# A fused recurrence and mixer on one core: the first low-rank product into two of four row groups, the second product for two chunks abreast, and a new order

## The chip, the cores and the metric

The kernel runs on one core of one Trainium2 chip (trn2). The metric is the time of one execution on the device in microseconds (us); the kernel before took 160.7 us, the median of three runs (160.70, 162.46 and 157.32).

## The reference

Four batches are computed, each with a sequence of 768 steps, 8 heads of width 48, so a model width of 384. A gated linear recurrence feeds a token mixer of rank 32 and a channel mixer with a hidden width of 1536:

```python
for t in range(S):                                    # S = 768
    state = alpha[:, :, t, :, None] * state + einsum('bhd,bhe->bhde', k[:, :, t], v[:, :, t])
    y[:, :, t] = einsum('bhd,bhde->bhe', q[:, :, t], state)
...
x = y as (batch, 768, 384)
h = x.transpose(0, 2, 1) @ U @ V                      # U: 768 x 32, V: 32 x 768
u = x + h.transpose(0, 2, 1)
out = u + maximum(u @ w_ch1, 0) @ w_ch2               # 384 x 1536 and 1536 x 384
```

## The kernel before

The sequence of each batch is cut into six chunks of 128 steps. Batches are numbered 0 to 3, and an operation is named here by its kind, its batch and its chunk (`mlp1 0.1.3`: batch 0, second half of the sequence, hidden block 3). Each batch goes through these stages:

- **Loads.** For each chunk one transfer each of alpha, k, q and v (192 KB) into one of 40 `io` tiles (`stage_loads`, lines 343 and 350). The weights of the channel mixer come over the same queue: twelve tiles of `w_ch1` of 192 KB (`weights1`, line 313), which are then cast into `w1_sb` by GpSimd or ScalarE (lines 265 and 269), and four pieces of `w_ch2` of 576 KB (`weights2`, line 328), which land in `h1t` and are cast from there into `w2_sb`. Three of the twelve tiles belong to one block of 384 hidden columns, that is to three of the twelve `mlp1` products of a half: tiles of block 0 to hidden blocks 0 to 2, of block 1 to 3 to 5, of block 2 to 6 to 8, of block 3 to 9 to 11.
- **Recurrence** (`stage_pair`, `stage_sums`, `stage_gla`). Logarithms of alpha are summed by a matmul (`pcum`, `cum`), exponentials of the sums scale k and q into `rkq` (`rk` and `rq`, lines 404 and 612, on GpSimd or VectorE), TensorE transposes these (`tr`, line 421), forms the scores (`psc`, `sc`), the state (`pd2`, `d`) and the result (`py`, `y`), and the result is copied from PSUM to `xb` (`pyev`, `yev`).
- **Token mixer** (`stage_mix`). The first low-rank product (`xu`, line 735) is one matmul for each of the six chunks, 128 rows by 32 columns, and it puts chunk c into column group c mod 4, so that one PSUM tile holds four partial sums of 32 rows each. One copy takes them to `utx` (128 x 384). The second product (`hb`, line 771) is one matmul per chunk over all 128 rows, against V repeated four times down the rows (`ve_sb`, `vm_sb`), so that this product also adds the four partial sums. VectorE adds the chunk of `xb` (`u`, line 772).
- **Channel mixer.** u is transposed, by TensorE in batches 0 and 1 (`utr`, line 791) and by the DMA queue in batches 2 and 3 (`tu`, line 777), then `mlp1` (line 820, three matmuls of 384 columns each), `relu` (lines 830 and 832), `mlp2` (line 846, twelve matmuls per chunk in three groups of four), the sum with u (line 852) and the store (line 857).

PSUM is used as eight banks. Each engine works through its own list in order, and waits at an instruction until what this needs is there. SyncE's list holds nearly all transfers. The order of all lists, the engine of each copy and the buffer of each tile are written out by hand: `Plan.add` collects the operations of all stages, and `Plan.run` issues them in the order of `TABLE`, three letters for one operation (two for its number, one for its engine), with `SLOTS` naming the buffers.

Of the kernel before, what the change touches and what calls it, by code (L numbers as in the profile page):

```python
# [13 lines left out]

CODE = "ABCDEFGHIJKLMNOPQRSTUVWXYZabcdefghijklmnopqrstuvwxyz0123456789+-"
TABLE = """
BDSA3AA7SA6AQLAA4SDeAA5SDgPBLSCXACZPBFSCuAA9SA8SCwPCYACaAAESCcACbADiAA+SCeDCzACyABESCdDEOAA-A++ECgPDlGCfPBHSCiDEQPBMSC1G
ChDDnPBGAETACxACmPDpABNSC0GCjPCnDDhABJSC3PERACkDAIGC2PCvABCACoPCqPClDC5AC9PDkGDFAC4DBASCpDESAC6PC+DBTSCrPEUGC7DC-PDmPBPA
DHPC8DDoADfGDBPBBSDIACsDEVGDCPDADDKADJADqPCtDBOSD3AEWPDDDDtPDEDDGGEXPDjADrDDUPD5PEZAEYDAJPD7ABIADuPDsDAKAEaPBKSDvDDLGEcD
BRSD+GGOABQADVPAMPGlADWDADSDNPDMGDwPD6AGQPDPDD8AANADXPDxDGnPGSADYDEPGDOPEbDGRABSSDyPD9GEdPDzPEAPGpADQDEePGoAD0PECDD4GGqA  # L20
DRPGTABUSD2AGVGD1AD-PEfDEgPBbADTDEGPEhPEBADZPEHPBVSDSDGUGDaPEDPBXSEIDDbPEEDAFGEiPBWADcAEKPGXPEkAEFDGWPDdAATSEJPGPAELPEjD
APSGYAGZDGdPGrGEMDElPARSENAGeDGaPHVAEmPGfDGhPGtPGbDEnAGsGAXSHXPGcDAVSEwPE2PHaAGvAE0PAZSExDGiPG8AEuPE1DBYSGmGGkAGuPGjAEqP
E3DAhSGwAEoPG+PEvDAdSAUAAQGE4PErDEpDAYGACGEyPEzDBaSBZSAfSAlSAjSG0PEsPAGPG1DAbSEtDASAHBAAaGAWGE5AFSPAAGHYAAHAG2DABDFUPG-A
HZAHAAFaPE6PFYPFCPFAPHCDFTAFZAFDDFVAFbAHEPFWPE7DHGDG9AHDGG3GE8PHFPE+PBjSFBAAgAAcAFEPFcPFFAAkAFXDE9DBfSBeSHHDHLPBcSBdSHIP
E-DGgGAmGBhSAnSBgSArSAvSAeGFiPFGPFIPHMDHNDAzSAOGHvAFdAHbGHRPFKPHJDAiAHKDFjAFHDHODHuAFJAHWABkSHcGFLDFmPFnDFkPFlABlSHQPHSP
HkPHUDHwPHlDHTAHmDHePHnDH1AIHAAqGHdPIGAApGHzAH0AHyAAoAH2GHfDHgAAsAAuGFoPFQPFpDFRDBrSBiSFePFgPFOPFhDFfAFPDFMPGxPHhPGzDHjD
AtAH3GBnSBmSBzSBoSFNAHiDHoGA0GBvSAxAAwAGIPAyGFwPH4PGyDH5PHpPGCPGJPHqPBpSH7AA1GH6DHPDH8PHrPF8PFxPIJDA2AF9PF+PH9DHtDH+DHxA
IIGILPHsDJ5AINAIKPIMDF-DFyPH-PFzDGKPJ6AIADIBDGDPGLDG4PIOPIPDIQDG5PJ7PJ+AJ9AKcAKOAKbAJ-AIDPIEDG6DKPAG7DBqSF2PICGIFGIRPISD
B3SGEPITPB1SBwSKdPF3PBxSGFDKMAIUAKNAB7SBySIjPKBGKCGKDSIkDALGKAABsSIbPIXPIVPF4PIdPKfAKwAKjGIWDIYDJ8AFqPKhAIhPFrPIZPIcDIeD
IfPKHPIiDIlPKiAKgAKxAKvAIaAKkGKyAFsPIgDI9PIxPIyAIrPIsAK+AF5DImDKIDI+DFtDK0DK-AJRPJSAJVPI-PJAAI5PI6AKQGJWDLAPLTABuSLSAKEP  # L30
KFDKGDKlSKmPLFALCAKLGJLPJFPKnDLEAB4SKeGLGGCHSJMALDAB5SLHDKWPKXDKoDCDSB2SB0SJHPJNPJJPJKDI3PI4DJODJIAB8SBtSKYGJPPI7PInPJDP
I1PKpPJGAI8AJEDKzDI2DLISB9SKJPKuAK1SKsPJBPKKAJCAIpPB6SNdAB-SM8AJQAIoAKtDIvPLUGKqDKrGIqAJTPK5PK6DJ0PJ1PKRGJvPLJPK2PJUDLKD
K3DLLDIzPI0AKSSK4DJ2PJwPJxPJyDIwAM7AItPLVGLBGLWSLMPK7GJ3DB+SK8PIuAK9ALNDLOGKTPM9PNAANRANBANCANQANOALXPJXPLPPLQACLSNeAKUD
KVDKZPJYPCESCMSLYDLZDLRGLaPJpPCASNSGCBSKaDLbALcPLdANfPJZPM-ANPANDGLjPN0ACGSNyALqPNzANkALlPNxACTSCFSLkDNEGN1GCCSNNAM+GLmD
LnSJqPLePLrDJrPLoPJjPJkPLfDLpDLsSLgPJdPJlPJePJfPN3PJsDN5ANYPNJPLhDJmDLiSCPSMTPMbPMVPNFSJgDNKDNTGNZDMUDNUSJaDMcDCJSCNSMWD
NhANiAMJPMKAODALvPLwACISLtPCQSMBPL7PLuDMCDOEAL8DMRPCVSMSANjANGPOFPNVPNHDNWDNIDObAOHAL9PL+ACKSOJACRSMLPMHPMIDMMAOaAMXPMNP
MFPL1PMODNmDNlDMYAL2ANnSL5PMZPMaAOIALzPMDPMGDN2GOLGNaGMPPL6DNXDMxPNgAONPN4PMQDNbPNrPN6DCUSNsDMEAL0AOKAL-PL3PMADCOSN7PNcA
OPDN9DNoPNpDFvSCSSJcSCWSN8DMyPL4ANwANLPOMGOdGOOPOfPLxPOQDOcGNMANtGLyAOePOgAMzPN+POBPORPOCAOGANqDOhDOiPN-DMiPOUPOTDOSDMjP
NuPM2POAGF7SOVDOZGOXPOjDNvAOkDOWGOlPM3POmAOYDOnPGHSFuSJnSGASJtSJuSF0SMsPMtPOoAOpPOrPOqDOuPMnPMkPOsDOtSOwPOvDMdPMlDOxDOyS
MePO1POzPO2DO0DM4PMuPMvDM0DMfPMoPMpPMqDM5DO4PPMPPGPPKPPOPO5APEPPLDPNAPFAJoSPPDMmSO3SJ4SMgDF6SPgPPcPPIPPQPPSPPdDPJAPTAPmP  # L40
PRAPnAPaPPkPO+PPbAPlAPUPPHAPVAMrSPWPPXDO6PPYPO7DPZDPhDMwSM6SJhSGBSJiSJbSJzSO8PO9DPCPPiPPAPPePO-APBAPjAPyPPtPP3PPoPPfAPDA
PzPPuPQBPGMSM1SP0PQCPMhSP1DF1SGNSP2SPpPQDPPvPPwDPxSPqPPrDPsSGGSQGPQHPQEDQIPQFSP4PQJDQKSP5PP6DP7SP8PP9PP+PP-DQAS
"""
# [94 lines left out]
def kernel(  # L138
# [42 lines left out]
    u_sb = const.tile([128, NC, R], BF16, name="u_sb")  # L181
# [3 lines left out]
    ue_sb = const.tile([128, NC, R], BF16, name="ue_sb")  # L185
# [148 lines left out]
    def paired(b, c):  # L334
        return c // 2 < PAIRS[b]
# [22 lines left out]
    def xk(b, xb, c):  # L358
        return [(xb, c, 0), (xb, c, 1)] if paired(b, c) else [(xb, c)]
# [369 lines left out]
    def stage_mix(b, xb, ub, uT):  # L729
        xu = Buf(bank)  # L730

        def f_utx(cs):
            for c in cs:
                g = c % 4
                nc.tensor.matmul(
                    xu()[32 * g : 32 * g + R, 0:DM], lhsT=(ue_sb if paired(b, c) else u_sb)[:, c, :], rhs=xb()[:, c, :],
                    start=(c < 4), stop=(c + 4 >= NC), skip_group_check=True,
                )
# [15 lines left out]
        def v_side(c):  # L754
            return (ve_sb if paired(b, c) else vm_sb)[:, c * C : (c + 1) * C]

        def f_hb3(c0):
            for g in range(3):
                rows = slice(32 * g, 32 * g + R)
                nc.tensor.matmul(hbs[c0 + g]()[:, 0:DM], lhsT=v_side(c0 + g)[rows], rhs=utx()[rows], start=True, stop=True)  # L760

        def v_keys(cs):
            return [("ve" if paired(b, c) else "vm", c // NT) for c in cs]

        for c in range(NC):
            hb = hbs[c]
            if b in ABREAST:
                if c % 3 == 0:
                    P.add(f"hb3 {b}.{c}", lambda e, c=c: f_hb3(c), r=[utx] + v_keys(range(c, c + 3)), w=hbs[c : c + 3])
            else:  # L770
                P.add(f"hb {b}.{c}", lambda e, c=c, hb=hb: nc.tensor.matmul(hb()[:, 0:DM], lhsT=v_side(c), rhs=utx(), start=True, stop=True), r=[utx] + v_keys([c]), w=[hb])  # L771
            P.add(f"u {b}.{c}", lambda e, c=c, hb=hb: nc.vector.tensor_tensor(ub()[:, c, :], xb()[:, c, :], hb()[:, 0:DM], op=ALU.add), r=[hb] + xk(b, xb, c), w=[(ub, c)])  # L772
# [144 lines left out]
```

## Time and profile before

| what | value |
|---|---|
| median of three runs | 160.7 us (157.32 to 162.46) |
| the profiled execution, its own time | 156.94 us |
| its span, first to last instruction | 155.0 us |
| what lies around the span | 1.94 us |
| TensorE busy | 146.3 us, 94% of the span, 1771 matmuls |
| VectorE, ScalarE, GpSimd busy | 109.1, 87.1 and 61.8 us |
| read from and written to HBM | 23.79 and 4.72 MB |

In the rows of the profile PE is TensorE, PEld its weight loads, DVE VectorE, ACT ScalarE, POOL GpSimd, and SPq the queue from which SyncE issues transfers. A row of the timeline has the start in us, the time from the first start to the last end of the merged instructions, the engine, the line, the operation with its tiles and shape, and how many were merged; in brackets stands how long the engine was idle before and what ended that. Matmuls overlap in TensorE's pipeline, so the pace of a stream is read from one start to the next and not from the length of one. A row of transfers has the line, the queue, the count, the size of one and the time from its issue to its landing.

### The profile page before, as it was taken

What the parts mean: (1) busy time and instruction counts of PE and PEld (TensorE: products, weight loads), DVE (VectorE), ACT (ScalarE), POOL (GpSimd) and SP (SyncE); (2) the same over time, 40 slices, a digit from 0 to 9 for tenths busy, and PEclk for the clock granted to TensorE, in tenths of its full rate; (3) what the DMA queues carried; (4) which work ended last, traced back from release to release, by engine and by line L of the source; (5) the groups of instructions that cost most, each with busy time, mean ns of one, the idle gap of its engine ahead of it and who ended that gap; (6) DMA issues with size and microseconds to landing.
All of it is one profiled execution on the core that took longest, in us unless ns stands there. A gap on an engine that the chain in (4) does not pass through costs nothing.

```text
span 155.0 us, 4552 instructions
## 1 busy us (share of the span) xinstructions
PE 146.3 (94%) x1771; PEld 97.6 (63%) x1771; DVE 109.1 (70%) x240; ACT 87.1 (56%) x225; POOL 61.8 (40%) x96
## 2 busy tenths in 40 slices
PE   0898999999999999999999999999999999999992
PEld 0567777666757675766657666666776555666661
DVE  6159999968989796879859665988897566160151
ACT  3858977988794549396636670775672103544000
POOL 8069886646557056254354473006553000000000
PEclk9999999999999999999999999999999999999999
DMA  4999999999998899999899997999984079760134
GB/s 120 323 325 323 270 287 343 307 340 244 338 351 183 183 209 228 159 221 230 151 216 198 184 234 133 199 204 187 191 210 121 9 172 160 240 218 0 51 125 161
DMA packets 94453, 32.35 MB, mean 209 GB/s; under 512 B 88128, under 2 KB 94400, under 8 KB 94432
## 3 DMA queue, kind: packets, MB, share of 16 engines
q1 hardware_dynamic: 89152, 30.09, 80.7%
q10 hardware_dynamic: 5280, 1.97, 4.9%
q8 instruction: 14, 0.23, 0.6%
q14 instruction: 7, 0.06, 0.1%
HBM read 23.79 MB, written 4.72 MB: 184 GB/s over the span
## 4 chain that ended last, share of the span: by engine, by line
PE 90%; DVE 5%; DMA 2%; issue 1%; POOL 1%; ACT 0%; DVEq 0%; POOLq 0%
PE ps L846 31%; PE ps L820 31%; PE ps L421 3%; PE ps L653 3%; DVE pm L456 2%; PE ps L445 2%; DMA io<-in_alpha_dram 2%; PE ps L771 2%; PE ps L720 2%; DVE ub L772 2%; PE ps L561 2%; PE ps L625 1%; PE ps L715 1%; PE ps L382 1%; PE ps L528 1%; PE ps L676 1%
## 5 line engine op out<-in xcount | busy, mean ns | idle before, releaser
L846 PE MATMUL ps<-w_sb,h1t 128*128 128x384 bf16 (+2 forms) x300 | 52.4, 320 | 0.0
L820 PE MATMUL ps<-uT,w_sb 128*128 128x384 bf16 x288 | 49.7, 326 | 0.0
L830 ACT ACTIVATE h1t<-ps 128x384 bf16<-128x384 f32 x56 | 25.7, 496 | 26.5 <-PE ps L820 26.2
L820 PEld LDWEIGHTS <-w_sb 128*128 128x128 bf16 x288 | 27.2, 98 | 17.6 <-DMA uT<-ub 0.4
L846 PEld LDWEIGHTS <-h1t 128*128 128x128 bf16 x300 | 27.5, 98 | 16.1 <-issue 0.3
L832 DVE TENSOR_SCALAR h1t<-ps 128x384 bf16<-128x384 f32 x40 | 20.8, 551 | 7.8 <-PE ps L820 7.7
L852 DVE TENSOR_TENSOR io<-ub,ps 128x384 f32<-128x384 bf16 (+2 forms) x25 | 12.9, 534 | 13.0 <-PE ps L846 12.7
L663 DVE TENSOR_TENSOR pm<-ps,maskc 128x512 bf16<-128x512 f32 x28 | 18.0, 683 | 2.9 <-PE ps L653 2.7
L772 DVE TENSOR_TENSOR ub<-xb,ps 128x384 bf16<-128x384 bf16 x24 | 11.9, 549 | 8.0 <-PE ps L771 8.0
L612 POOL TENSOR_TENSOR rkq<-io,ai 128x384 bf16<-128x384 f32 x12 | 11.1, 924 | 14.0 <-ACT ai L601 5.1
L612 POOL TENSOR_TENSOR rkq<-io,aa 128x384 bf16<-128x384 f32 x10 | 9.1, 913 | 10.8 <-DMA io<-in_q_dram 9.6
L456 DVE TENSOR_TENSOR pm<-ps,maskp 128x512 bf16<-128x512 f32 x20 | 12.9, 683 | 0.7 <-PE ps L445 0.5
L687 POOL TENSOR_TENSOR st<-sm,tot 128x384 bf16<-128x384 f32 x9 | 7.8, 864 | 11.1 <-DVE sm L703 9.0
L265 ACT COPY kqt<-ps 128x512 bf16<-128x512 bf16 x13 | 7.8, 596 | 6.2 <-DMA uT<-ub 4.7
L404 POOL TENSOR_TENSOR rkq<-io,aa 128x384 bf16<-128x384 f32 x9 | 8.3, 931 | 6.8 <-ACT aa L397 4.0
L265 ACT CAST xb<-ps 128x192 bf16<-128x192 f32 (+1 forms) x18 | 6.9, 405 | 5.1 <-PE ps L720 4.2
L269 POOL CAST rv<-io 128x384 bf16<-128x384 f32 x12 | 6.3, 529 | 6.2 <-DMA io<-in_v_dram 5.0
L602 ACT ACTIVATE aa<-ps 128x384 bf16<-128x384 f32 x14 | 7.0, 501 | 3.0 <-PE ps L570 3.0
L267 DVE COPY kqt<-ps 128x512 bf16<-128x512 bf16 x17 | 7.1, 419 | 2.2 <-PE ps L421 0.9
L404 POOL TENSOR_TENSOR rkq<-io,ai 128x384 bf16<-128x384 f32 x8 | 7.2, 907 | 2.9 <-PE ps L445 1.2
L421 PE MATMUL ps<-ident,rkq 128*128 128x128 bf16 x80 | 7.7, 229 | 0.7 <-DVE pm L456 0.4
L382 PE MATMUL ps<-lt,upto 128*128 128x384 bf16 x10 | 3.9, 392 | 4.5 <-ACT lt L373 4.5
(114 smaller groups left out, 218.7 us busy)
## 6 DMA issues: line engine op xcount, KB each, us to landing
io<-in_q_dram SPq DMA_DIRECT2D x24, 192.0 KB, 4.3
io<-in_k_dram SPq DMA_DIRECT2D x22, 192.0 KB, 4.3
io<-in_alpha_dram SPq DMA_DIRECT2D x20, 192.0 KB, 4.3
io<-in_v_dram SPq DMA_DIRECT2D x20, 192.0 KB, 4.1
out_dram<-io SPq DMA_DIRECT2D x13, 192.0 KB, 2.1
io<-in_moe_w_ch_dram SPq DMA_DIRECT2D x12, 192.0 KB, 4.7
h1t<-in_moe_w_ch_dram SPq DMA_DIRECT2D x4, 576.0 KB, 7.0
out_dram<-io SPq DMA_DIRECT2D x20, 96.0 KB, 2.2
```

The source lines that it names most:

```text
L265: nc.scalar.copy(dst, src)
L404: eng.tensor_tensor(jh(dst()[:, :, 0:D]), raw(a), jh(x()), op=ALU.mult)
L421: nc.tensor.matmul(dst, lhsT=ring()[:, HP * j + 2 * a : HP * j + 2 * a + 2, :].rearrange("t h w -> t (h w)"), rhs=ident, start=True, stop= ...
L456: nc.vector.tensor_tensor(dst, s2, maskp.to_broadcast([C, 2, 2, C]), op=ALU.mult)
L612: eng.tensor_tensor(dst()[:, :, 0:D], a(), x(), op=ALU.mult)
L663: nc.vector.tensor_tensor(pm()[:, :, par, :], s2, maskc.to_broadcast([C, HP, C]), op=ALU.mult)
L772: P.add(f"u {b}.{c}", lambda e, c=c, hb=hb: nc.vector.tensor_tensor(ub()[:, c, :], xb()[:, c, :], hb()[:, 0:DM], op=ALU.add), r=[hb] + xk( ...
L820: nc.tensor.matmul(hb()[:, 0:TW], lhsT=w1_sb[:, ct, jt * 128 : (jt + 1) * 128], rhs=u_half(uT, ct, tt, b in QUEUE_U), start=(ct == 0), sto ...
L830: nc.scalar.activation(dst, hb()[:, 0:TW], AF.Relu)
L832: nc.vector.tensor_scalar_max(dst, hb()[:, 0:TW], 0.0)
L846: nc.tensor.matmul(hb()[:, 0 : hi - lo], lhsT=h1()[:, jt, c * C : (c + 1) * C], rhs=w2_sb[:, jt, lo:hi], start=(jt == 0), stop=(jt == NJ - 1),
L852: P.add(f"out_{hi - lo} {b}.{c}", lambda e, hb=hb, lo=lo, hi=hi: nc.vector.tensor_tensor(flat(ou)[:, lo:hi], ub()[:, c, lo:hi], hb()[:, 0 ...
```

## The change

All four batches get the new form (`TWICE`). In the first product each chunk is now multiplied twice, into column groups c mod 2 and c mod 2 + 2: twelve matmuls instead of six, and groups 0 and 2 hold the sum over the even chunks, groups 1 and 3 that over the odd ones. So rows 0 to 63 of `utx` hold both partial sums, and rows 64 to 127 hold them again. The second product then takes 64 rows for one chunk: `f_hb2` issues two matmuls, for chunk c on rows 0 to 63 and for chunk c + 1 on rows 64 to 127, into two PSUM banks. There are three such pairs per batch, 24 matmuls in all as before. `SLOTS` and most of `TABLE` are new: the lists of the engines are the same up to the first product of batch 0 and differ from there on, in order and also in which engine does a copy, a cast or a scaling.

```diff
+    TWICE = (0, 1, 2, 3)
...
         def f_utx(cs):
             for c in cs:
-                g = c % 4
-                nc.tensor.matmul(
-                    xu()[32 * g : 32 * g + R, 0:DM], lhsT=(ue_sb if paired(b, c) else u_sb)[:, c, :], rhs=xb()[:, c, :],
-                    start=(c < 4), stop=(c + 4 >= NC), skip_group_check=True,
-                )
+                n = 2 if b in TWICE else 4
+                for g in range(c % n, 4, n):
+                    nc.tensor.matmul(
+                        xu()[32 * g : 32 * g + R, 0:DM], lhsT=(ue_sb if paired(b, c) else u_sb)[:, c, :], rhs=xb()[:, c, :],
+                        start=(c < n), stop=(c + n >= NC), skip_group_check=True,
+                    )
...
+        def f_hb2(c0):
+            for g in range(2):
+                rows = slice(64 * g, 64 * g + 64)
+                nc.tensor.matmul(hbs[c0 + g]()[:, 0:DM], lhsT=v_side(c0 + g)[rows], rhs=utx()[rows], start=True, stop=True)
...
+            elif b in TWICE:
+                if c % 2 == 0:
+                    P.add(f"hb2 {b}.{c}", lambda e, c=c: f_hb2(c), r=[utx] + v_keys(range(c, c + 2)), w=hbs[c : c + 2])
```

One row of the new table beside the old one, the first in which they differ by more than the numbers of the operations:

```diff
-APSGYAGZDGdPGrGEMDElPARSENAGeDGaPHVAEmPGfDGhPGtPGbDEnAGsGAXSHXPGcDAVSEwPE2PHaAGvAE0PAZSExDGiPG8AEuPE1DBYSGmGGkAGuPGjAEqP
+EMDElPENAGWAGoGGpGABGEmPEnAGaPGbDGcDGVAEtPAPSGqPEuDG5AEvDEyPEzDE0DGrPEoPARSEpDEqDG7PGsAGXPEwPE1PAXSAVSBZSE2DGYDGdGAUGAQG
```

Three places of the new lists follow, all three in the stretch in which batch 0 goes through its channel mixer and batch 1 through its recurrence. The first is SyncE's queue, transfers 45 to 55 in its order; `in_moe_w_ch` into an `io` tile is a tile of `w_ch1`, into `h1t` a piece of `w_ch2`. Before:

```order
L343 DMA io_143<-in_k_dram 128x4x96
L343 DMA io_146<-in_q_dram 128x4x96
L350 DMA io_147<-in_q_dram 128x8x48
L328 DMA h1t_73<-in_moe_w_ch_dram 128x3x384
L350 DMA io_145<-in_k_dram 128x8x48
L328 DMA h1t_73<-in_moe_w_ch_dram 128x3x384 x3
L350 DMA io_148<-in_k_dram 128x8x48
L350 DMA io_150<-in_q_dram 128x8x48
L343 DMA io_151<-in_alpha_dram 128x4x96
```

And with the change:

```order
L344 DMA io_143<-in_q_dram 128x4x96
L329 DMA h1t_73<-in_moe_w_ch_dram 128x3x384
L344 DMA io_146<-in_k_dram 128x4x96
L329 DMA h1t_73<-in_moe_w_ch_dram 128x3x384
L314 DMA io_147<-in_moe_w_ch_dram 128x384
L351 DMA io_145<-in_q_dram 128x8x48
L329 DMA h1t_73<-in_moe_w_ch_dram 128x3x384 x2
L314 DMA io_148<-in_moe_w_ch_dram 128x384
L351 DMA io_150<-in_k_dram 128x8x48
L344 DMA io_151<-in_alpha_dram 128x4x96
```

The last two of the twelve tiles of `w_ch1` (`io_147` of block 3, `io_148` of block 2) now stand among and behind the pieces of `w_ch2`, as transfers 49 and 53, where all twelve were within the first 41 before; and `io_146`, now behind the first piece of `w_ch2` as transfer 47, holds k of chunk 2 of batch 1, which was transfer 33 (`io_132`) before.

The second place is GpSimd's list in the same stretch, from the `trij` copy on. Before:

```order
L269 COPY trij<-h1t_73 64x256
L404 TENSOR_TENSOR rkq_81<-io_137,aa_177 128x8x48
L494 TENSOR_TENSOR st_196<-sm_195,tot_183 128x192
L494 TENSOR_TENSOR st_197<-sm_194,tot_186 128x192
L269 CAST w_sb<-io_138 128x384
L269 CAST w_sb<-io_134 128x384
L302 COPY vm_sb<-ve_sb 128x384
L404 TENSOR_TENSOR rkq_80<-io_143,ai_182 128x8x48
L404 TENSOR_TENSOR rkq_80<-io_146,aa_178 128x8x48
```

And with the change:

```order
L270 COPY trij<-h1t_73 64x256
L270 CAST w_sb<-io_138 128x384
L405 TENSOR_TENSOR rkq_81<-io_171,aa_178 128x8x48
L270 CAST rv_175<-io_165 128x384
L270 CAST w_sb<-io_137 128x384
L270 CAST w_sb<-io_141 128x384
L270 CAST w_sb<-io_148 128x384
L270 CAST w_sb<-io_139 128x384
L495 TENSOR_TENSOR st_196<-sm_195,tot_185 128x192
L405 TENSOR_TENSOR rkq_80<-io_136,ai_180 128x8x48
```

GpSimd now casts five tiles of `w_ch1` nearly in a row here, among them `io_138` (transfer 39, block 1) and `io_148` (transfer 53, block 2), and the tile `io_139` (block 2) and the scalings of chunk 3 of batch 1 stand behind `io_148`.

The third place is VectorE's list where the first `relu` of batch 0 (into `h1t_72`) stand. Before:

```order
L267 COPY uT_208<-ps 128x2x3x128
L508 TENSOR_TENSOR sm_195<-ps,st_196 128x192
L267 COPY trij<-h1t_73 64x256
L404 TENSOR_TENSOR rkq_81<-io_132,ai_180 128x8x48
L832 TENSOR_SCALAR h1t_72<-ps 128x384 x2
```

And with the change:

```order
L268 COPY uT_208<-ps 128x2x3x128
L457 TENSOR_TENSOR pm_192<-ps,maskp 128x4x128
L843 TENSOR_SCALAR h1t_72<-ps 128x384
L405 TENSOR_TENSOR rkq_81<-io_146,ai_182 128x8x48
L843 TENSOR_SCALAR h1t_72<-ps 128x384 x3
```

The scaling of k of chunk 2 of batch 1 (`rk 1.2`) still stands among the first `relu`, three of which are behind it, and it now reads `io_146`. On TensorE the transpose of this `rkq` (`tr 1.2`) comes after eight `mlp1` products with the change and came after seven before; the first product on block 1 of the weights (`mlp1 0.0.5`) is now the fifth, and the first on block 2 (`mlp1 0.1.6`) the sixteenth.

63 lines of the change are left out of this document (32 added, 31 removed).

## The prediction

> **What bounds the kernel now.** I read the page first, its busy times, the rate of the transfers and the chain that ended last:
>
> ```profile
> span 155.0 us, 4552 instructions
> ...
> PE 146.3 (94%) x1771; PEld 97.6 (63%) x1771; DVE 109.1 (70%) x240; ACT 87.1 (56%) x225; POOL 61.8 (40%) x96
> ...
> GB/s 120 323 325 323 270 287 343 307 340 244 338 351 183 183 209 228 159 221 230 151 216 198 184 234 133 199 204 187 191 210 121 9 172 160 240 218 0 51 125 161
> ...
> PE 90%; DVE 5%; DMA 2%; issue 1%; POOL 1%; ACT 0%; DVEq 0%; POOLq 0%
> ```
>
> TensorE is 90% of the chain. The transfers run at 240 to 350 GB/s from the second to the twelfth slice (4 to 46 us) and near 200 after. The busy time by stretches and the end of TensorE's timeline say how full TensorE is:
>
> ```profile
> 30.60:45.40 14.80, 14.80 (x159) 9.38 (x156) 12.52 (x29) 12.59 (x34) 8.04 (x14) 1.00 1.07 320
> 45.40:151.80 106.40, 106.40 (x1125) 69.46 (x1124) 72.70 (x139) 51.33 (x130) 32.79 (x43) 1.00 0.80 173
> ```
>
> ```profile
> 147.77 4.17 PE L846 MATMUL ps<-w_sb,h1t 128*128 128x384 bf16 x35
> ```
>
> From 30.6 us, where the first mlp1 starts, to its last matmul at 151.8, TensorE has no idle time at all (the second and third numbers of a row are the length and TensorE's busy time). So two things count: how much TensorE has to do, and any wait that the new order puts into it, since nothing gives a lost microsecond back. Between 30.6 and 45.4 the transfers are full too (share 1.07, 320 GB/s): there, what TensorE waits for can be a transfer.
>
> **The work of TensorE.** The mix of batch 2, by its timeline, and two plain matmuls of 192 columns:
>
> ```profile
> 88.55 0.50 PE L735 MATMUL ps<-xb,u_sb 128*32 128x384 bf16 x6
> 88.98 0.50 PE L561 MATMUL ps<-lt,trij 64*128 64x192 bf16 x8
> 89.32 0.34 PE L570 MATMUL ps<-ones,lt 64*128 64x1 bf16 x16
> 89.60 0.82 PE L846 MATMUL ps<-w_sb,h1t 128*128 128x384 bf16 x4
> 90.26 0.65 PE L771 MATMUL ps<-utx,vm_sb 128*128 128x384 bf16 x3
> 90.75 0.81 PE L846 MATMUL ps<-w_sb,h1t 128*128 128x384 bf16 x4
> ```
>
> ```profile
> 28.58 0.24 PE L383 MATMUL ps<-lt,below 128*128 128x192 bf16 x1
> 28.66 0.24 PE L384 MATMUL ps<-lt,upto 128*128 128x192 bf16 x1
> ```
>
> Three hb take 90.75 - 90.26 = 0.49, 0.163 each, with nothing lost on entering or leaving. The six xu take 0.43 = two rounds of 0.163 and 0.10: four column groups run abreast, and the change of shape to the next line costs about 0.10. Matmuls on 64 rows do run abreast: eight of 192 columns take 0.34 (88.98 to 89.32), 0.04 each, where one on 128 rows takes 0.08.
>
> So, for all four batches: the second product drops from 24 to 12 steps of 0.163 (-1.96); the first goes from two rounds to three in each batch (+0.65); and pairs on 64 rows among products on 128 pay for the change of shape. Counted along TensorE's two lists, the changes of shape go from 64 to 68 (some pairs stand beside other 64-row work): +0.4. Sum: -0.9 us. Bounds: no more than -1.6 if a switch into a pair is free, and +1.0 if the pairs don't run abreast. Weight loads stay beside the matmuls. Here a rule of the Trainium skill bears on it (TensorEngine Tiling (Array Packing), Tiling Modes, Key Properties): changing the tiling mode drains TensorE. The 0.10 behind xu agrees; by that rule a pair alone among 128-row products saves about nothing (0.163 against two switches).
>
> **The waits of the new order.** Transfers are issued and land in the order of the queue, and SyncE stops issuing when too many are under way. SyncE's timeline and, for four issues, the transfers in a stretch around each (in the last column the time to landing):
>
> ```profile
> 29.10 1.89 SPq L313 DMA_DIRECT2D io<-in_moe_w_ch_dram  x4
> ...
> 35.25 0.68 SPq L350 DMA_DIRECT2D io<-in_q_dram  x1
> 36.09 1.01 SPq L328 DMA_DIRECT2D h1t<-in_moe_w_ch_dram  x1
> 37.69 2.97 SPq L328 DMA_DIRECT2D h1t<-in_moe_w_ch_dram  x3
> 40.70 0.72 SPq L350 DMA_DIRECT2D io<-in_k_dram  x1
> ```
>
> ```profile
> io<-in_moe_w_ch_dram SPq DMA_DIRECT2D x1, 192.0 KB, 4.6
> ```
>
> ```profile
> io<-in_q_dram SPq DMA_DIRECT2D x1, 192.0 KB, 3.8
> ```
>
> ```profile
> h1t<-in_moe_w_ch_dram SPq DMA_DIRECT2D x1, 576.0 KB, 5.5
> ```
>
> ```profile
> io<-in_k_dram SPq DMA_DIRECT2D x1, 192.0 KB, 7.6
> ```
>
> The first of these four is transfer 39 (the second of the four from 29.10, so issued near 29.65), the second 47, the third 48, the last 53. They landed at 34.3, 39.1, 41.6 and 48.3 us. By then, before, all twelve tiles of w_ch1 were long there: the last of them is the fourth of the row at 29.10. The new queue has the same bytes ahead of places 39 and 53 (the same four pieces of w_ch2 and the same count of small transfers), and two small ones' bytes more ahead of place 47. So with the change: io_138 (a tile of block 1) lands at 34.3; io_146 (k for rk 1.2) between 39.1 and 41.6, I take 40.7; io_148 (a tile of block 2) at 48.3.
>
> What waits for them, by the rows of GpSimd, VectorE and TensorE:
>
> ```profile
> 30.05 0.96 POOL L269 CAST w_sb<-io 128x384 bf16<-128x384 f32 x2 [0.18 <-DMA io<-in_moe_w_ch_dram]
> ```
>
> ```profile
> 31.87 0.56 DVE L404 TENSOR_TENSOR rkq<-io,ai 128x384 bf16<-128x384 f32 x1
> ```
>
> ```profile
> 30.64 3.59 PE L820 MATMUL ps<-uT,w_sb 128*128 128x384 bf16 x21
> 34.07 0.39 PE L421 MATMUL ps<-ident,rkq 128*128 128x128 bf16 x4
> 34.29 1.14 PE L820 MATMUL ps<-uT,w_sb 128*128 128x384 bf16 x6
> ...
> 37.05 0.34 PE L479 MATMUL ps<-rv,rkq 64*128 64x96 bf16 x8
> ...
> 37.67 1.64 PE L820 MATMUL ps<-uT,w_sb 128*128 128x384 bf16 x9
> ...
> 40.87 0.37 PE L528 MATMUL ps<-rv,pm 64*128 64x48 bf16 x16
> 41.09 0.33 PE L479 MATMUL ps<-rv,rkq 64*128 64x96 bf16 x8
> 41.26 0.65 PE L561 MATMUL ps<-lt,trij 64*128 64x192 bf16 x8
> ...
> 41.95 0.62 PE L421 MATMUL ps<-ident,rkq 128*128 128x128 bf16 x8
> ```
>
> One mlp1 is three matmuls of 0.163, 0.49 us (21 in 34.07 - 30.64). TensorE begins mlp1 of batch 0 near 30.6 as before. The four products on block 0 last to 32.6; the fifth needs io_138, at 34.3 plus one cast (0.48): **a first wait** of some 2 us. Four more products, to 36.8; then tr 1.2 needs rk 1.2, which VectorE can do when io_146 is there: 40.7 + 0.6 = 41.3, **a second wait** of 4.5 us. VectorE is held at rk 1.2 all that time, with three relu behind it, and these free the banks for the next products; GpSimd is held at io_148 from about 37 on, with the scalings of batch 1 behind it. After tr 1.2 TensorE finds seven products and 1.7 us of other work, which the queued relu spread out; the sixteenth product needs io_148 and io_139 cast, two casts behind 48.3: **a third wait**, to 48.3 + 0.96 = 49.3.
>
> What is lost is counted at 49.3, since a wait there covers those before it. TensorE has done by then fifteen mlp1 (7.3), two tr 1.2 (0.44), py 1.0 (0.22, from 40.87 to 41.09), cum1 1.4 (0.69, 41.26 to 41.95), pd2 and psc 1.2 (0.62, 37.05 to 37.67): 9.3. Before it had done 49.3 - 30.6 = 18.7. Of the 9.3, 0.6 (pd2 1.1, py 1.0 and uperm) had been done before 30.6 in the old order. So it is 18.7 - 8.7 = 10.0 behind. Of the saving, what belongs to batches 1 to 3 is still to come: 3 x (0.49 - 0.163) = 0.98, less three changes of shape (0.3), 0.7. Net +9.3 us. That of batch 0 is without effect, since the queue sets 49.3.
>
> Once past this, the transfers are ahead of a later TensorE, and in the mixes of batches 1 to 3 there is 1.1 us or more of mlp2 and mlp1 between the first product and the second, and 2 to 6.5 us between the second and what needs its sums, against six additions of u on VectorE: I put no further wait there. Six PSUM banks at once for the pairs of batch 3 are paid by the same cover.
>
> **The forecast.** 156.94 + 9.3 = 166.2 on the profiled execution's own time. The median shown is 3.8 above that execution, and I don't know what those runs spent it on; I take half: **168.0 us**. The likeliest case's own range is 164 to 171: the landing of io_146 and io_148 within 1.5 us, a backlog on GpSimd of up to 2, and the 3.8. Slower by over 2%, about what a measurement of this kernel can tell from no change: 0.89.
>
> **Rivals.**
>
> *Only the second wait binds* (0.18): the tiles of block 2 come earlier than place 53 suggests. At 41.3 TensorE has done eight products (3.9, less 0.6) where it had done 10.7: 7.4 behind, less 0.7: 163.6, with half of the 3.8 165.5. For it, the times to landing of the four pieces of w_ch2 (least, median, most) are uneven; against it, landing follows the bytes ahead.
>
> ```profile
> DMA to landing us min/median/max: 5.5/7.0/8.7
> ```
>
> *The clock falls in the second wait* (0.14). TensorE starts slow in this trace:
>
> ```profile
> 4.50 0.48 PE L382 MATMUL ps<-lt,upto 128*128 128x384 bf16 x1 [4.50 <-ACT lt L373]
> ...
> 9.33 0.53 PE L382 MATMUL ps<-lt,upto 128*128 128x384 bf16 x1
> ...
> 26.28 0.33 PE L382 MATMUL ps<-lt,upto 128*128 128x384 bf16 x1
> ```
>
> The same matmul takes 0.48 to 0.53 in the first 5 us of work and 0.33 later. If a wait of 4.5 us puts TensorE back to that, 5.5 us of work run at half pace: up to 2.7 us more, 168.9, with half of the 3.8 170.8. Against it, much of that would fall into the time before the third wait. The Trainium skill says so (TensorE: Matmul & The Clock Gate, Part 1): after an idle window of about 3.4 us the clock is halved; no wait in this trace after the start is long enough to show it.
>
> *No wait: the tiles come in time* (0.09). This one ends on the other side: only the work counts, 156.94 - 0.9 = 156.0, within 2%. It decides if the queue is faster than its consumers, that is if io_148 lands by 38.9, when the fifteen products and the rest (9.3 from 30.6, less the casts) would be done. Transfers 27 to 53 are 23 x 192 + 4 x 576 KB = 6.9 MB; issued from 22 us, that needs 408 GB/s. The highest slice of the page has 351. With the runs' 3.8 it is 159.8.
>
> *The change doesn't do what it says* (0.02): the pairs run one after the other. Then hb2 saves nothing, 1.5 us more in batches 1 to 3: 167.7, with half of the 3.8 169.6.
>
> In another 0.07 the waits are those of the forecast and others of the new order add to them. **Chances**: the forecast 0.50 (0.57 with those); faster by over 2% 0.02 (out of the third rival), same 0.09, slower 0.89. The range that holds the time 8 times in 10 is 161 to 174: from below the lone second wait to the clock's case with the whole 3.8.
>
> **What would show it.** In the profile after, TensorE's slices between 30 and 50 us are no longer full: waits before L831 of about 2 us ended by GpSimd's cast, before L422 of about 4 ended by VectorE's L405, and before L831 near 49 again by GpSimd; GpSimd waits some 10 us for a tile of w_ch1; from 52 us on TensorE is full as before. The second product shows 12 pairs that start together, 0.16 to 0.36 us each. Wrong it is if TensorE is full from 31 us on, if transfer 47 lands before 36 us, or if the time is below 161.

## The result, and the profile after

The changed kernel took 169.77 us in the median (168.39 to 170.64), the kernel before on the same chip 160.7 (157.32 to 162.46, five runs by now): ratio 1.0755, 95% interval 1.063 to 1.088, slower. The ratio compares fast runs alone, which are 157.32 and 158.09 of the kernel before (the other three, 160.70 to 162.46, count as slow) and all five of the changed kernel. Each ratio below is taken in the same way, against the kernel before on the same chip, where its median was 157.6 to 158.1.

The page of the changed kernel (span, TensorE's forty slices of 4.2 us, and in tenths the granted clock in them, that is the share of its full clock that TensorE was given):

```profile
span 168.9 us, 4598 instructions
...
PE   0988799916298999999999999999999999999992
...
PEclk9999789996569999999999999999999999999999
```

TensorE is no longer full from 30 us on: the slices from 34 to 46 us read 1, 6 and 2, and from 38 to 51 us the granted clock is down as well. From 54 us to the end it is full again, as before. The waits of the changed kernel (engine and line, what it waited for, total, times, longest):

```profile
POOL w_sb L270 <- DMA io<-in_moe_w_ch_dram: 17.1, 2, 11.1
DVE rkq L405 <- DMA io<-in_k_dram: 11.0, 1, 11.0
...
PE ps L422 <- DVE rkq L405: 4.4, 1, 4.4
PE ps L831 <- POOL w_sb L270: 4.0, 1, 4.0
...
PE ps L831 <- DVE sm L509: 0.7, 1, 0.7
```

These are the three waits of the forecast, at the lines and for the operations named there: TensorE's first mlp1 on block 1 behind GpSimd's cast, tr 1.2 behind VectorE's scaling of k, and the products on block 2. They in turn stand behind transfers. TensorE's timeline has their places (start, length, engine, line, operation, what ended the idle time before):

```profile
31.97 2.44 PE L831 MATMUL ps<-uT,w_sb 128*128 128x384 bf16 x14
38.45 2.68 PE L831 MATMUL ps<-uT,w_sb 128*128 128x384 bf16 x10 [4.05 <-POOL w_sb L270]
45.56 0.61 PE L422 MATMUL ps<-ident,rkq 128*128 128x128 bf16 x4 [4.43 <-DVE rkq L405]
...
53.56 1.62 PE L831 MATMUL ps<-uT,w_sb 128*128 128x384 bf16 x9 [0.71 <-DVE sm L509]
```

A gate is here the moment at which what TensorE waits for is there. The third gate, which the forecast put at 49.3 us, opened at 53.56. How, say GpSimd's rows, VectorE's and SyncE's:

```profile
51.69 0.96 POOL L270 CAST w_sb<-io 128x384 bf16<-128x384 f32 x2 [11.07 <-DMA io<-in_moe_w_ch_dram]
52.61 0.51 POOL L495 TENSOR_TENSOR st<-sm,tot 128x192 bf16<-128x192 f32 x1
```

```profile
53.15 0.36 DVE L509 TENSOR_TENSOR sm<-ps,st 128x192 f32<-128x192 f32 x1 [2.03 <-POOL st L495]
```

```profile
44.79 1.33 SPq L314 DMA_DIRECT2D io<-in_moe_w_ch_dram  x1
```

Transfer 53 was issued at 44.79 (the transfer in place 53 before: 40.70) and landed near 51.6, just before GpSimd began its cast. Then TensorE needed more than the two casts: the state (L495) stands behind them on GpSimd, VectorE's sum (L509) waits for the state, and the PSUM bank that this sum empties is the one the next mlp1 writes. From there to the end hardly more is lost. The first mlp1 of batch 1, before and after:

```profile
64.86 3.41 PE L820 MATMUL ps<-uT,w_sb 128*128 128x384 bf16 x20
```

```profile
78.44 0.81 PE L831 MATMUL ps<-uT,w_sb 128*128 128x384 bf16 x4
```

It begins 13.6 us later, and the span is 13.9 us longer.

### The profile page after: what moved, and what is told of

Read it like the earlier page. It is cut to its first block, busy times and chain, and to the rows that moved or that the text cites. A ratio compares the mean times of both kernels' runs of the same rounds, so it can differ in the third digit from the quotient of the medians.

```text
span 168.9 us, 4598 instructions
## 1 busy us (share of the span) xinstructions
PE 149.2 (88%) x1795; PEld 97.6 (58%) x1795; DVE 111.3 (66%) x243; ACT 84.9 (50%) x218; POOL 62.6 (37%) x100
## 2 busy tenths in 40 slices
DMA packets 94453, 32.35 MB, mean 191 GB/s; under 512 B 88128, under 2 KB 94400, under 8 KB 94432
## 4 chain that ended last, share of the span: by engine, by line
PE 75%; DMA 11%; issue 5%; POOL 3%; ACT 2%; DVE 2%; POOLq 0%; SPq 0%; DVEq 0%; ACTq 0%
PE ps L857 28%; PE ps L831 25%; DMA io<-in_k_dram 7%; DMA io<-in_alpha_dram 4%; PE ps L422 2%; PE ps L654 2%; PE ps L721 2%; PE ps L737 2%; PE ps L529 1%; PE ps L562 1%; PE ps L626 1%; PE ps L716 1%; POOL w_sb L270 1%; PE ps L768 1%; PE ps L480 1%
## 5 line engine op out<-in xcount | busy, mean ns | idle before, releaser
L831 PE MATMUL ps<-uT,w_sb 128*128 128x384 bf16 x288 | 52.6, 334 | 4.8 <-POOL w_sb L270 4.0
L841 ACT ACTIVATE h1t<-ps 128x384 bf16<-128x384 f32 x50 | 23.7, 492 | 38.5 <-PE ps L831 38.3
L843 DVE TENSOR_SCALAR h1t<-ps 128x384 bf16<-128x384 f32 x46 | 23.7, 551 | 10.3 <-PE ps L831 10.2
L613 POOL TENSOR_TENSOR rkq<-io,aa 128x384 bf16<-128x384 f32 x10 | 9.5, 951 | 10.3 <-ACT aa L603 8.1
L266 ACT CAST xb<-ps 128x192 bf16<-128x192 f32 (+1 forms) x22 | 8.0, 390 | 9.9 <-PE ps L721 7.3
L266 ACT COPY kqt<-ps 128x512 bf16<-128x512 bf16 x17 | 9.9, 589 | 4.5 <-PE ps L626 2.9
L688 POOL TENSOR_TENSOR st<-sm,tot 128x384 bf16<-128x384 f32 x6 | 5.0, 828 | 18.5 <-DVE sm L704 18.5
L270 POOL CAST w_sb<-io 128x384 bf16<-128x384 f32 x9 | 4.3, 505 | 17.1 <-DMA io<-in_moe_w_ch_dram 17.1
L422 PEld LDWEIGHTS <-rkq 128*128 128x128 bf16 x80 | 5.5, 105 | 8.4 <-DVE rkq L405 5.4
L602 ACT ACTIVATE ai<-ps 128x384 bf16<-128x384 f32 x14 | 7.0, 501 | 4.0 <-PE ps L571 3.3
L405 DVE TENSOR_TENSOR rkq<-io,ai 128x384 bf16<-128x384 f32 x2 | 1.1, 556 | 11.0 <-DMA io<-in_k_dram 11.0
```

The lines of the kernel that those rows point to most:

```text
L266: nc.scalar.copy(dst, src)
L405: eng.tensor_tensor(jh(dst()[:, :, 0:D]), raw(a), jh(x()), op=ALU.mult)
L422: nc.tensor.matmul(dst, lhsT=ring()[:, HP * j + 2 * a : HP * j + 2 * a + 2, :].rearrange("t h w -> t (h w)"), rhs=ident, start=True, stop= ...
L613: eng.tensor_tensor(dst()[:, :, 0:D], a(), x(), op=ALU.mult)
L831: nc.tensor.matmul(hb()[:, 0:TW], lhsT=w1_sb[:, ct, jt * 128 : (jt + 1) * 128], rhs=u_half(uT, ct, tt, b in QUEUE_U), start=(ct == 0), sto ...
L841: nc.scalar.activation(dst, hb()[:, 0:TW], AF.Relu)
```

## The experiments

Two questions: does the last of the gates alone make the time, or do the waits, and the clock in them, add up; and what are the pairs worth without the new order.

### The loads: which gate counts

In four kernels only SyncE's list is another, in the places of transfers 32 to 53 or 54 (the numbers are the changed kernel's places):

```diff
-32 33 34 35 36 37 38 39 40 41 42 43 44 45 46 47 48 49 50 51 52 53       (the change)
+47 32 33 34 35 36 37 38 39 40 41 42 43 44 45 46 48 49 50 51 52 53       (k of 1.2 early)
+39 32 33 34 35 36 37 49 40 42 53 38 44 45 46 47 43 48 50 41 51 52       (tiles early)
+39 47 32 33 34 35 36 37 38 40 41 42 43 44 45 46 48 49 50 51 52 53       (last gate left)
+39 47 32 33 34 35 36 37 49 40 42 53 38 43 44 45 46 48 50 51 52 41       (all early)
```

**k of 1.2 early.**

> The new order and mix, with the k load io_146 alone moved from place 47 of the queue to place 32, the tiles of w_ch1 left late. Theory A (the waits cover each other, the last one sets the loss): the second wait, before tr 1.2, goes, and TensorE waits longer for io_148 instead; the time falls by less than 1.5 us, ratio 1.06 to 1.08. Rival D (each wait costs its own length): 4.4 us less than the change, ratio near 1.045.

Measured: 168.94 us, ratio 1.0725 (1.0645 to 1.0804). Taking the second wait away gives nothing, as theory A said. The longer wait for `io_148` that it named is not in the trace, though: the first wait is there with 4.3 us, and the next is one of 3.9 us behind a relu of ScalarE, of which the run after the next one tells more.

**Tiles early, k left.**

> The new order and mix, with the late tiles of w_ch1 moved ahead of the pieces of w_ch2 and the k load io_146 left at place 47. Theory A: the first and the third wait go, the second stays and grows (TensorE reaches tr 1.2 earlier, k lands no earlier): TensorE is then 6 to 7 us behind at tr 1.2, ratio 1.035 to 1.05. Rival E (the third wait alone sets the time): back to before, ratio 1.00 to 1.02.

Measured: 167.17 us, ratio 1.0601 (1.0514 to 1.0687). With the first and the third gate gone, this is all that stands in TensorE's waits beyond its start, 1.2 us for k and q and two of 0.2 and 0.3:

```profile
PE ps L422 <- DVE rkq L405: 6.8, 1, 6.8
```

The second gate took over most of what the third had covered. The wait is about what theory A said (TensorE 6 to 7 us behind), but the time lies above its range. A reason is in the trace: the gate opened at 42.0 us, and behind it, from 42.0 to 45.1, the granted clock was 0.50.

**First two early, last gate left.**

> The changed kernel with transfers 39 and 47 (the tile of the first wait, the k of the second) moved to places 32 and 33, and transfer 53 (the last tile of w_ch1) left at place 53. Theory A (only the last gate counts: whatever TensorE loses before it is covered by the wait for transfer 53): the first two waits go to under 1 us each, the third grows to 6 to 9 us, TensorE goes on at 51 to 53.5 us as in the change, and the time stays within 1.5 us of it, 168 to 171, ratio 1.06 to 1.08. Theory E (the three waits add up): 8.5 us of waits less, 161 to 163, ratio 1.02 to 1.035.

Measured: 168.48 us, ratio 1.0663 (1.0583 to 1.0743). The time is that of theory A, but not the row that A expected. The waits show one wait of 10.3 us, and ScalarE's timeline what it hangs on:

```profile
PE ps L562 <- ACT h1t L841: 10.3, 1, 10.3
```

```profile
46.18 0.51 ACT L266 CAST w_sb<-io 128x384 bf16<-128x384 f32 x1 [11.46 <-DMA io<-in_moe_w_ch_dram]
46.59 0.48 ACT L841 ACTIVATE h1t<-ps 128x384 bf16<-128x384 f32 x1
```

ScalarE casts a tile of block 3 too, transfer 49, and a relu stands behind that cast whose bank TensorE needs. In the changed kernel ScalarE sat at the same cast, hidden under the second wait:

```profile
46.89 0.51 ACT L266 CAST w_sb<-io 128x384 bf16<-128x384 f32 x1 [7.17 <-DMA io<-in_moe_w_ch_dram]
```

TensorE went on at 47.13 and met the third gate without a wait that the profile shows. Its products and VectorE's sum, which opens that gate:

```profile
48.90 5.36 PE L831 MATMUL ps<-uT,w_sb 128*128 128x384 bf16 x24
```

```profile
52.21 0.36 DVE L509 TENSOR_TENSOR sm<-ps,st 128x192 f32<-128x192 f32 x1 [2.43 <-POOL st L495]
```

At a granted clock of 0.50 from 47.6 to 51.0 us the 24 matmuls took 5.2 us in place of 3.9, so that TensorE came to the sixteenth product just when the third gate opened, near 52.6. This run alone does not tell the third gate from ScalarE's and the slow clock behind it; the run with the clock kept, below, does.

So there are four gates, and taking away any that isn't the last only lets the next be seen.

**All early.**

> The new order and the new mix, with SyncE's transfers 32 to 53 in another sequence alone: the late tiles of w_ch1 (io_138, io_139, io_141, io_147, io_148) and the k load io_146 go ahead of all pieces of w_ch2. Theory A: the three waits of TensorE between 32 and 54 us go, and the time comes back to that of before, ratio 0.98 to 1.02. Rival C (the new lists lose time elsewhere too, by other waits of their own): 2 us or more above before, ratio 1.02 to 1.05.

Measured: 163.07 us, ratio 1.0355 (1.0299 to 1.0412): half of the loss is back, so theory A missed and rival C holds. What was left had one large row of its own:

```profile
PE ps L857 <- POOL w_sb L270: 3.8, 1, 3.8
```

mlp2 waits for a cast of `w_ch2`, and ahead of that cast GpSimd's list has the scaling of k of chunk 1.4, whose transfer (place 50) was now late. Moving that k ahead of the four pieces of `w_ch2`:

```diff
-39 47 32 33 34 35 36 37 49 40 42 53 38 43 44 45 46 48 50 51 52 41 54    (all early)
+39 47 32 33 34 35 36 37 49 40 42 53 38 45 43 44 50 46 48 51 52 54 41    (by need)
```

> The changed kernel with transfers 32 to 54 in the order in which TensorE's list first needs them; against the earlier run with the loads moved back, the k tile of chunk 1.4 (place 50) stands ahead of the four triple tiles of w_ch2, because GpSimd's scaling of it stands in GpSimd's list ahead of the casts of those tiles, which made a wait of 3.83 us there. Theory A (with every load in time the new order is no longer than the old): that wait falls under 1 us, 159 to 161, ratio 1.005 to 1.022. Rival C (the new order asks for more bytes sooner than the queue can bring them, so that one wait is only traded for another): 162 to 164, ratio 1.03 or more.

Measured: 162.76 us, ratio 1.0311 (1.0249 to 1.0372), span 159.7. Theory A missed, and rival C's number holds: the wait of 3.8 became 1.6, and others grew. That the queue can't bring the bytes soon enough, as rival C has it, is not shown by that. TensorE's waits, first of this kernel, then of the kernel before, each without the 4.5 us at the start, and of this kernel without three of 0.2 to 0.3:

```profile
PE ps L831 <- ACT kqt L266: 1.6, 1, 1.6
PE ps L857 <- POOL w_sb L270: 1.6, 1, 1.6
PE ps L422 <- POOL rkq L405: 1.0, 2, 0.7
```

```profile
PE ps L421 <- DVE pm L456: 0.4, 1, 0.4
PE ps L421 <- POOL rkq L404: 0.2, 1, 0.2
```

With the small ones that is 4.9 us of waits for 0.6, and the span is 4.7 us longer. The order of the loads is worth some six tenths of the loss (7.55% to 3.11%). The rest must be in what else is new, the lists of the other engines, the buffers in `SLOTS` and the mix; the runs below price the mix, but nothing here tells the lists from the buffers. No order of loads tried here brought the kernel level with the one before.

### The clock

The granted clock by stretches of 3.4 us (the stretch, its length, busy times of PE, PEld, DVE, ACT and POOL with the number of instructions, the clock, the share and rate of the transfers), in the changed kernel:

```profile
15.30:18.70 3.40, 2.11 (x47) 1.54 (x47) 2.65 (x6) 2.52 (x8) 2.07 (x4) 1.00 1.11 298
18.70:22.10 3.40, 3.40 (x33) 2.67 (x32) 2.10 (x6) 2.32 (x8) 3.38 (x6) 0.50 1.09 266
...
35.80:39.20 3.40, 0.75 (x5) 0.49 (x6) 0.00 (x0) 0.37 (x1) 1.31 (x2) 1.00 0.87 214
39.20:42.60 3.40, 1.93 (x7) 0.60 (x5) 0.00 (x0) 0.52 (x2) 1.42 (x4) 0.50 0.99 261
42.60:46.00 3.40, 0.44 (x4) 0.45 (x5) 1.06 (x3) 0.00 (x0) 0.00 (x0) 0.50 1.10 349
46.00:49.40 3.40, 3.40 (x37) 2.04 (x36) 2.03 (x5) 2.51 (x7) 0.00 (x0) 0.50 1.04 331
```

TensorE had half its clock for 13.6 us in all, with some 9 us of work in them, and ahead of each of the four slow stretches stands one in which it was busy 62% or less. A low share doesn't always bring it on, though; in the same trace, behind this stretch the clock stayed at 1.00:

```profile
32.35:35.76 3.41, 2.05 (x13) 1.02 (x11) 1.60 (x4) 2.32 (x6) 0.00 (x0) 1.00 1.01 298
```

The slow stretches looked like the 4.4 us by which the profiled execution lies above the forecast's sum. To test it, the gaps were filled with work that changes nothing: products already in PSUM are computed again (operations named here in place of their numbers; the two `psc` aim at the stretch from 15.30 to 18.70, which the expectation puts at 14 to 17.5).

```diff
+REPEAT = {mlp1 0.0.1: 9, mlp1 0.0.3: 9, mlp1 0.0.2: 2, psc 0.5: 3, psc 0.3: 2}
...
-            op.fn({"P": "PE", "A": "ACT", "D": "DVE", "G": "POOL", "S": "SP"}[table[n + 2]])
+            for _ in range(REPEAT.get(op.i, 1)):
+                op.fn({"P": "PE", "A": "ACT", "D": "DVE", "G": "POOL", "S": "SP"}[table[n + 2]])
```

> The changed kernel, with TensorE kept busy in its waits by repeating products that are done already: mlp1 0.0.1 nine times in place of once (8 x 0.49 = 3.9 us of the first wait of 4.05), mlp1 0.0.3 nine times (3.9 of the second wait of 4.43), mlp1 0.0.2 twice, and two score products of batch 0 two and three times in the stretch from 14 to 17.5 us, where TensorE was busy 2.11 of 3.40 us. No load and no list moves, so the gates stand at the same landings. Theory A (the clock falls because of the idle stretches, and costs 3 to 4.5 us behind them): the granted clock is 1.00 or has one fall of 3.4 us left, and the time comes down by 2.5 to 4.5 us although more work is done, 165 to 167, ratio 1.045 to 1.06. Rival D (the falls lie inside the waits and cost nothing, or come anyway): 169 to 171, ratio 1.07 to 1.08.

Measured: 169.64 us, ratio 1.0737 (1.0669 to 1.0805), with a granted clock of 0.997 to 1.00 in all six runs (0.96 to 0.98 in those of the change). Theory A falls: the clock was kept, and the time did not move. A row of its waits, four lines further down in its code, shows why:

```profile
PE ps L835 <- DVE sm L513: 2.1, 1, 2.1
```

What a faster TensorE gained ahead of the third gate, it spent waiting there: 2.1 us in place of 0.7. The gate itself opened at 52.83, since GpSimd's cast waited for transfer 53 as before, and from it to the first mlp1 of batch 1 it is 24.9 us in either kernel:

```profile
50.96 0.96 POOL L274 CAST w_sb<-io 128x384 bf16<-128x384 f32 x2 [12.91 <-DMA io<-in_moe_w_ch_dram]
```

### The mix by itself

**The new order with the mix of before.** Each pair is two single products again, the first product has six matmuls:

```diff
 xup4 0, xup2 0, xup 1, xup 2, xup 3      ->  xu4 0, xu2 0, xu 1, xu 2, xu 3
-hb2 0.2
+hb 0.2, hb 0.3                           (and so for all twelve pairs)
```

> The lists of the change with the mix of before: each pair is issued as its two single products at the pair's place, and the first product is not doubled. Theory A (the order of the loads makes the loss, the mix is worth a few tenths either way): the three waits stand where they stood, since none of them hangs on the mix, and the time is that of the change within 1 us, 169 to 171, ratio 1.065 to 1.08. Theory B (the new mix itself costs some 3 us, as it did in the old order): 166 to 167, ratio 1.04 to 1.06.

Measured: 170.08 us, ratio 1.07 (1.06 to 1.08), so the order makes the loss and theory B falls. That the times agree so closely is in part chance. In this kernel's trace the third gate opened 1.5 us sooner than in the changed kernel, and the nine matmuls behind it took 2.35 us in place of 1.62:

```profile
52.08 2.35 PE L820 MATMUL ps<-uT,w_sb 128*128 128x384 bf16 x9 [2.01 <-DVE sm L508]
```

From 52.8 to 56.2 us the granted clock was 0.50. Here the fall lay behind the last gate, where nothing covers it, and it cost about 1.5 us: from that gate to the first mlp1 of batch 1 it is 26.4 us, in the changed kernel 24.9. Past the waits, where both traces are at full clock, the two mixes can be read against each other: first the kernel with the old mix, then the changed one, the starts of mlp1 of batches 1 and 3 (that of batch 1 in the changed kernel, 78.44, stands above):

```profile
78.50 0.81 PE L820 MATMUL ps<-uT,w_sb 128*128 128x384 bf16 x4
...
142.35 1.95 PE L820 MATMUL ps<-uT,w_sb 128*128 128x384 bf16 x11
```

```profile
142.08 2.11 PE L831 MATMUL ps<-uT,w_sb 128*128 128x384 bf16 x12
```

63.85 us with the old mix, 63.64 with the new, and two mixes lie between: 0.10 us a batch. The kernels with other loads or the repeats have the new mix as well and take 63.62 or 63.63 there, but two of them (k early, last gate left) take 63.33, which would be 0.26 a batch.

**The old order with the new mix**, three times. First, each pair at the place of its first single product:

```diff
-hb 0.3 ... hb 0.5 ... hb 0.4 ... hb 0.2 ... hb 0.1 ... hb 0.0
+hb2 0.2 . hb2 0.4 ................... hb2 0.0
```

> The new mix alone: the lists of before, with each chunk's first product in two column groups and the three pairs of the second product, each pair at the place of the first hb of its two chunks (the copies' and casts' engines and the queue as before). Theory A (the new order's late transfers cost the time, the mix itself saves a little): 0.9 us less than before, ratio 0.985 to 1.005. Rival B (the 64-row pairs themselves cost the time, by changes of shape, by PSUM banks held in twos or by running one after the other): most of the 9 us stays, ratio 1.03 or more. A pair alone between 128-row products should take 0.35 us in the timeline if the change of shape costs 0.10 on either side.

Measured: 161.41 us beside 158.06, ratio 1.0232 (1.0162 to 1.0302). Theory A missed by more than 4 us, and rival B asked for more than this; the time lies between the two. TensorE's waits:

```profile
PE ps L768 <- DVE ub L783: 0.8, 2, 0.5
PE ps L831 <- DVE h1t L843: 0.7, 1, 0.7
```

The pairs (L768) wait for VectorE to empty a bank. So the pairs were spread over the places of the first, third and fifth single product, with the adds in their order; 36 tiles, the pairs' and some of other products, got other PSUM banks by that:

```diff
+hb2 0.4 ......... hb2 0.2 ......... hb2 0.0
```

> The lists of before with the new mix, as in the first of these runs, but the three pairs of a batch stand at the places of the first, third and fifth single product, and the residual adds follow in the pairs' order, so that no pair needs its second bank before VectorE has emptied it. Theory A (the 3.6 us of the first such run were waits of a pair for a bank or for the adds, 0.33, 0.33 and 0.48 us with the pipe refilled behind each, and two waits of mlp1 of 0.65 and 0.42 behind late adds; the products themselves gain: pairs 2.82 us in place of 4.05, the doubled first product 2.61 in place of 1.85): those waits go, 157.5 to 159 beside 158 of before, ratio 0.995 to 1.008. Theory B (pairs and row groups cost that much by themselves): 161 to 162, ratio 1.018 to 1.025.

Measured: 161.88 us, ratio 1.0269 (1.0217 to 1.032). Theory A missed again, with other waits (mlp1 for relus, sums and adds), and the time is theory B's 161 to 162; that its reason isn't theory B's, the next two kernels show. They tell the mix from the banks: the new mix with every bank as before, and the kernel before with nothing new but the banks of that run.

```diff
 new mix, banks of before: each pair at the place of a later single product, where both its banks are free
-hb 1.5 ... hb 1.2 hb 1.1 hb 1.0 hb 1.3 ... hb 1.4
+.......................... hb2 1.0 hb2 1.2 hb2 1.4
 old mix, other banks: SLOTS alone, 37 of 704 letters, all of them PSUM banks
-... FBHBCBCGCDFCHBAGAFCAAGDFDEJBK ...
+... FBHBCBCGCDFCHBAFAGAACGDDFEJBK ...
```

> The lists of before with the new mix, once more, but with every PSUM bank as in the kernel before: each pair stands where its second single product stood or just behind, so that both its banks are those that the single products had, and the residual adds keep their places on VectorE (two of them one or two places later). Theory A (the mix costs next to nothing by itself: with the lists of the change, the doubled first product and the pairs come 0.10 us sooner in a batch than the old mix; what the first two such runs lost were waits for PSUM banks, 2.2 and 4.4 us in the trace, since a pair takes two banks at once and the moved pairs changed who shares a bank with whom): 157 to 158.5 beside 157.5 to 158 of before, ratio 0.993 to 1.005. Theory B (pairs and row groups cost 3 us by themselves in this order): 161 or more, ratio 1.02 or more.

Measured: 158.67 us beside 158.09, ratio 1.0061 (1.0023 to 1.0099). Theory B falls; theory A's range ends at 1.005, just below.

> The kernel before, untouched in its lists and its mix, with the PSUM banks of the run whose pairs were spread: 37 of its 704 slots get another number, nothing else. Theory A (who shares a bank with whom costs that run most of its 4.2 us): some of its waits of mlp1 for VectorE's relu or adds appear here too, 159 to 161.5, ratio 1.01 to 1.025. Theory B (the banks are innocent, the mix is the cost): within 0.5% of before.

Measured: 162.78 us, ratio 1.0308 (1.0251 to 1.0365). That is more than theory A said, and theory B falls: the banks alone cost 3%, and most of the waits of the spread pairs are here without a pair:

```profile
PE ps L820 <- DVE h1t L832: 1.1, 1, 1.1
...
PE ps L820 <- DVE io L852: 0.6, 1, 0.6
PE ps L846 <- DVE ub L772: 0.6, 2, 0.3
```

With the old banks the mix is left with its own price, some 1 us in the old order (0.4 to 1.6 by the interval). TensorE's timeline of that kernel has lone pairs between groups of mlp2:

```profile
60.84 0.82 PE L857 MATMUL ps<-w_sb,h1t 128*128 128x384 bf16 x4
61.60 0.34 PE L768 MATMUL ps<-utx,ve_sb 64*128 64x384 bf16 x2
61.87 0.82 PE L857 MATMUL ps<-w_sb,h1t 128*128 128x384 bf16 x4
```

From the first group of mlp2 to the second it is 1.03 us, and the four products themselves take 0.65: a lone pair costs 0.38, more than the two single products in its place (0.33). In the changed kernel, pairs stand beside each other and beside other 64-row work:

```profile
70.66 0.51 PE L737 MATMUL ps<-xb,ue_sb 128*32 128x384 bf16 x8
70.99 0.34 PE L737 MATMUL ps<-xb,u_sb 128*32 128x384 bf16 x4
71.26 1.47 PE L857 MATMUL ps<-w_sb,h1t 128*128 128x384 bf16 x8
72.67 0.50 PE L768 MATMUL ps<-utx,ve_sb 64*128 64x384 bf16 x4
73.00 0.49 PE L562 MATMUL ps<-lt,trij 64*128 64x192 bf16 x8
```

Two pairs take 0.33 there (72.67 to 73.00), half of four single products. The Trainium skill (TensorEngine Tiling (Array Packing), Tiling Modes, Key Properties) says that changing the tiling mode drains TensorE; these rows agree, with about 0.1 us on either side of a lone pair.

## Why the prediction was right

**The sign and the mechanism** were right: the kernel is slower by waits of TensorE for the transfers that the new list puts later, at the three places named. Of the rivals, "no wait" is out, "only the second wait binds" is out since the time stayed with that wait gone, and "the pairs run one after the other" is out since the two matmuls of a pair share one row of 0.34 us where two in sequence take 0.49.

**"What is lost is counted at 49.3, since a wait there covers those before it"** was the sound step. Freeing the second wait gave nothing, freeing the first two next to nothing, a kept clock nothing; only kernels that moved transfer 53 gained. They moved transfer 49 too, and 53 was never moved alone, so the row that shows this gate to be the last is the 2.1 us that TensorE waits at it when its clock is kept.

**The gates' times** were mis-sized. Counted by bytes and places, transfer 53 was to land at 48.3 and the gate to open at 49.3; in the trace it landed near 51.6 and the gate opened at 53.56. The 4.3 us between 49.3 and 53.56 are nearly the whole difference between the sum for the profiled execution (166.2) and its own time (170.64). 3.3 of them are a later landing: a place in the list is issued only when SyncE gets there, 44.79 here and 40.70 before, and SyncE too waits for landings and freed buffers. The same bytes stood ahead of place 53, as the forecast had counted, but its landing times took for granted that the queue comes to them as fast as before, and it did not: from 22 to 32 us the transfers ran at 246 GB/s, before at 319, and in that stretch SyncE waited 2.6 us at one go for the landing of an alpha load, where before none of its waits from 22 to 47 us is over 0.9. What else made its issues later was not taken apart. The other 1.0 is a chain the forecast left out, from the cast over GpSimd's state and VectorE's sum to a bank. The first mlp1 began at 31.97 and not near 30.6, and the first two waits were 4.05 and 4.43 us for 2 and 4.5, all without effect on the end.

**A gate was missed**: ScalarE's cast of transfer 49, which held its relus until 47.3 us. It lay under the others and cost nothing here.

**The median came out near by luck in part.** The half of the 3.8 us that the forecast added for the median proved no part of the change: the changed kernel's profiled execution lies 0.9 above its median, where that of before lay 3.8 under. These 1.9 us made up for some of the 4.4 by which the sum was short. Between the profiled executions the loss is 13.7 us, and the forecast had 9.3.

**The rival of the clock** gave 170.8, nearer to 169.77 than the forecast's 168.0, and the clock did fall, for longer than it said. It is still not the reason: with the clock kept, the time is the same. Its own objection, that much of it falls into the time before the third wait, was right. Nearest of all, with 169.6, was the rival of pairs that run one after the other, and the rows of the pairs rule it out; a time alone tells little of its cause.

**The work of TensorE** was put at -0.9 us, 0.23 a batch; it measured 0.10 a batch in the new order, and 0.26 by the two kernels with 63.33. The first product's third round is right (0.60 from 70.66 to 71.26 with the change of shape, 0.43 before, 0.16 forecast). Where the saving is 0.10, the term for changes of shape, 0.4, was too small: a lone pair pays about 0.1 twice and gains nothing. Of the 0.7 us that was still to come in batches 1 to 3, nothing is left at the end: the loss is 13.6 us at the first mlp1 of batch 1, behind the first of these mixes, and 13.9 over the span.

**"I put no further wait there"** held in the changed kernel: none of TensorE's waits there is in the mixes of batches 1 to 3 with more than 0.3 us, and between mlp1 of batch 1 and of batch 3 the new mix came out shorter. It would not have held for the same mix in the old order, where the kernels with these pairs were over 2% slower until the pairs had the old banks.

What stays open: which of the further moves in the new lists, or which of the new buffers, make the last 3% that remain with the loads by need. Its waits are named above; none was tried alone, and nor was the changed kernel with other banks. No kernel tried here was faster than the one before; the nearest has its order and banks with the new mix, at 1.0061.

## What to carry to other kernels

Where several waits stand in a row on one engine, the last gate makes the time: work out when each opens, and take away the last first, or all. A slower clock ahead of that gate was covered by it here, and one behind it was paid for. A transfer's landing is read from when its queue gets to issue it, not from the bytes ahead of it alone. When a written-out order is changed, keep the buffers of everything that does not change: here 37 other PSUM banks cost 3%, more than the edit in question could bring or take.

## What was not expected of the hardware

TensorE's clock fell to half not only after a wait of 4 us, but also after a stretch of 3.4 us in which it was busy 2.11 us with no gap over 0.9 us, and it stayed there for 3.4 us, once for three times that. With repeated products in that stretch, busy 2.52 us of it, no fall followed. The busy share alone doesn't decide, since the stretch from 32.35 to 35.76, busy 2.05 us and then idle, was followed by full clock; what does was not tested. In the kernel before, the least busy such stretch behind its start was followed by none either:

```profile
10.06:13.47 3.41, 2.73 (x73) 2.09 (x73) 2.53 (x6) 3.15 (x9) 2.51 (x3) 1.00 1.17 323
```

The Trainium skill (TensorE: Matmul & The Clock Gate, Part 1) has the window of 3.4 us and the half rate after an idle one. That a stretch still busy for 62% can bring it on, and one busy for 60% not, is what this trace adds.
